# Attention rows kept turned into the MLP: the sums' reciprocals applied by a product, the mean taken out of the weights

## The chip, the cores and the metric

The kernel runs on one core of a Trainium2 chip. It has five engines with a queue each: PE (TensorE, matrix products; PEld is its weight load), DVE (VectorE), ACT (ScalarE), POOL (GpSimd) and SP (SyncE, which here only issues transfers). The metric is the device time of one execution in microseconds. The kernel before took 1570.1 us (median of 3 runs, 1569.33 to 1570.96).

## The reference

Attention over 8 batches and 8 heads of 576 rows and 64 columns, in which each row keeps its 32 largest scores, then a channel MLP with a residual on the 4608 rows of 512 columns that the heads give side by side.

```python
scores = scale * np.matmul(q, k.transpose(0, 1, 3, 2))
kth = np.partition(scores, -top_k, axis=-1)[..., -top_k:-top_k + 1]
scores = np.where(scores >= kth, scores, -1000000000.0)
scores = scores - np.max(scores, axis=-1, keepdims=True)
attn = np.exp(scores)
attn = attn / (np.sum(attn, axis=-1, keepdims=True) + 1e-09)
x = np.matmul(attn, v)                        # heads side by side: (8, 576, 512)
...
mu = np.mean(x, axis=-1, keepdims=True)
var = np.mean((x - mu) ** 2, axis=-1, keepdims=True)
xn = (x - mu) / np.sqrt(var + 1e-06) * g_ln
ch = np.maximum(xn @ w_ch1, 0.0) @ w_ch2      # 512 -> 2048 -> 512
return x + ch
```

q, k, v and g_ln are float32; the two weights come as float64 and are turned into float32 on the chip.

## The kernel before

**Units, groups, jobs.** A unit is 128 rows of scores for a pair of heads (or the last 64 rows of both heads, a *rest*). A job is one batch and one pair of heads with the row tiles worked on together; its units are its group. There are 160 units in 80 groups, in a written order: the first jobs have two whole units, in between stand jobs of a single rest, later ones have two whole units and a rest. Four jobs (the four pairs of heads) give the 512 columns of the same rows.

**A step.** A loop over steps n writes out each engine's instructions by hand, nothing is reordered later, and each queue runs in that order. In step n PE makes the scores of unit n+2 (`scores`, L438), ACT copies them out of PSUM (L419), DVE picks the 32 largest of unit n in four rounds (`select`, L483, L469, L475), with `halve` (L461, L462) ahead of the next unit. For unit n-1 ACT and POOL make the mask (`mask`, L532 on ACT, L535 on POOL) and ACT the exponential with its row sum (`weigh`, L543), which lands in the group's tile `den`; L555 adds the small constant. The weights are then turned: by PE and copies (`turn`, L606), or for "moved" units by a DVE transpose of 32x32 blocks (L577), a write to HBM (L594) and four reads back into `pt` (`bring`, L587). Some steps after its last unit, `lag`, a group meets the values: `values` (L669, L677) gives `av`, rows on the columns, head dimensions on the partitions.

**From values to the MLP.** `take_values` (L687) copies `av` to `oT`. `place` turns each 128 rows back on PE (L714) and ACT scales both heads' halves by the reciprocals in `den` (`put`, L691; the reciprocal is L1350 on DVE) into the tile `x`, rows on the partitions. Rests are gathered over two batches first (L705 on POOL), their sums moved by two small transfers (`keep_den`, L659), and are turned by `place_rest` (L721). When the four pairs are there, two tiles make a `Block` of 256 rows. `stats` (L742, L743) takes mean and variance on DVE, and POOL subtracts the mean from x (L748, L751; for the first block DVE does, L745). `turn_x` turns the centred rows again on PE (L778, copied by L781) into `xT`. Then come the hidden products (L819, ACT's relu L842) and the projection: plain for the first two blocks (L858), afterwards by the scheme of seven products in place of eight (`seven`, L979) with sums on POOL (L909 to L915, L959, L963). `finish` scales by the inverse deviation (L797), adds x (L790, POOL) and stores (L793).

**The planner.** PE's products of the blocks stand in a list `todo` of turns, hidden and projection products, with a cost each. Eight times in a step `fill` takes as many as the step's share allows (`slot`: the shares are evened out up to the next block, by costs per step, not by time). `give` puts a new block into the list: its turns ahead of the last ten projection products of the block before, its hidden products behind them. Turns wait until their rows are centred. Sums, ends, stores and transfers are put off by a number of fills (`Later`).

**Weights.** The 32 pieces of 128x512 are fetched and converted in steps -1 to 21 beside the attention: ACT (L164, L166, L169), POOL (L165, and for the first matrix L171, which multiplies the sign by the gain g), DVE (`shift`, L177), POOL (`join`, L183, L185). After that POOL makes the seven-product forms of the second matrix.

Of the kernel before, what the change touches and what calls it, by code (L numbers as in the profile page):

```python
# [21 lines left out]
J = 4  # L22
# [7 lines left out]
def compute(  # L30
# [52 lines left out]
    xtpool = pool("xt", 1)  # L83
# [26 lines left out]
    hi_homes = [const([P, 2, HALF + (1 if doubt is None else 2) * LOWS], f"hi{i}") for i in range(2)]  # L110
    ident = const([P, P], "ident")
    make_identity(nc, ident[:])
    columns = const([P, J + NC], "columns")
    half, gcol = columns[:, 0:J], columns[:, J : J + NC]
    nc.gpsimd.memset(half[:], -0.5)
    w1 = const([P, NC, DFF], "w1")
# [6 lines left out]
    class Piece:  # L123
# [22 lines left out]
        def fetch(self):  # L146
            self.raw = xpool.tile([P, DM, 2], U32, tag="x", name="raw")
            nc.sync.dma_start(self.raw[:].rearrange("p n w -> p (n w)"), self.src)

        def split(self):  # L150
            i = self.i
            high = self.raw[:, :, 1].bitcast(FP32)
            if i < 3 * NC:
                self.size = hpool.tile([P, DM], U32, tag="h", name="size")[:]
                self.low = wt_rows[:, i % 8]
                homes = ((opool, "o"), (opool, "o"), (rpool, "r"), (rpool, "r"), (xtpool, "xT"))
            else:
                self.size = wt_rows[:, 2 * i % 8].bitcast(U32)
                self.low = wt_rows[:, (2 * i + 1) % 8]
                homes = ((opool, "o"), (opool, "o"), (rpool, "r"))  # L160
# [9 lines left out]
            if self.i < NF:  # L170
                nc.gpsimd.tensor_scalar(  # L171
                    self.sign[:], self.sign[:], gcol[:, self.c : self.c + 1], 1.0,
                    ALU.mult, ALU.mult,
                )
# [6 lines left out]
        def join(self):  # L181
# [4 lines left out]
            ready[self.i] = now[0]  # L186
# [3 lines left out]
    ready = [None] * (2 * NF)  # L190
    pieces = [Piece(i) for i in range(2 * NF)]
# [3 lines left out]
    def load_gain():  # L195
        ps = turned()
        nc.tensor.transpose(ps[:, 0:NC], grow[:], ident[0:NC, 0:NC])
        nc.scalar.copy(gcol[:], ps[:, 0:NC])

# [337 lines left out]
    def weigh(u, t):  # L537
        g = u.group
        if g.den is None:
            g.den = denpool.tile([P, 2 * J + 1], FP32, tag="den", name="den")  # L540
        col = 2 * u.qt + t
# [5 lines left out]
        if u.rest:  # L547
            den = g.den[:, 2 * J : 2 * J + 1]
        elif u.weighed == 2 and u is [x for x in g.units if not x.rest][-1]:
            whole = [qt for qt in g.qts if qt < J]  # L550
            den = g.den[:, 2 * whole[0] : 2 * whole[-1] + 2]
            g.sums = den
        else:
            return
        nc.scalar.activation(den, den, AF.Copy, bias=DEN_EPS)  # L555
# [94 lines left out]
    xs, xps, rs, oTr, dr = {}, {}, {}, {}, {}  # L650
# [612 lines left out]
    for n in range(END):  # L1263
# [24 lines left out]
        if g and not quick:  # L1288
            values(g)
# [187 lines left out]
```

## Time and profile before

| | |
|---|---|
| runs | 1570.1 us (median of 3), 1569.33 to 1570.96 |
| profiled execution | 1571.11 us, its span 1569.2 us |
| granted clock of PE, mean over the span | 0.975 |
| PE, PEld busy | 1469.0 us (94%), 1108.0 us (71%) |
| DVE busy | 1363.4 us (87%) |
| ACT busy | 1083.8 us (69%) |
| POOL busy | 981.2 us (63%) |
| transfers | 374774 packets, 245.60 MB |

Busy times are shares of the whole span; the kernel has stages with different limits, so the prediction reads them by stretches. In a line of groups stand the source line, the engine, the operation, out<-in, the shapes and the count, then the busy time, the mean of one in ns, and the idle time of the engine just before with what ended it. In a timeline line stand start and length, the engine, line and tiles, and how many like it follow. PE's ends are modelled, and a product in float32 has two records.

### The profile page before, as it was taken

The page shows a single profiled execution, that of the slowest core. Times are in us where ns is not written, and L with a number is a line of the kernel's source. Part 1 is how long each engine was busy: PE and PEld are TensorE (multiplying, and loading weights), DVE is VectorE, ACT ScalarE, POOL GpSimd, SP SyncE. Part 2 cuts the span into 40 slices and gives each one's busy share as a digit, 9 for nine tenths or more (in the row PEclk, how much of TensorE's full clock was granted, in tenths as well). Part 3 has the DMA queues.
Part 4 walks back from the last instruction along what each step waited for, and adds up shares of the span by engine and source line. Part 5 has one row for each costly group of instructions (what it writes and reads, how often), then busy time and mean ns, then how long its engine had stood idle before and what let it go on. Part 6 is the DMA issues. An engine that isn't in the chain of part 4 may idle for free. (4 is left out here: it accounts for less than half of the span.)

```text
span 1569.2 us, 27215 instructions
## 1 busy us (share of the span) xinstructions
PE 1469.0 (94%) x8046; PEld 1108.0 (71%) x8046; DVE 1363.4 (87%) x3873; ACT 1083.8 (69%) x3081; POOL 981.2 (63%) x1318
## 2 busy tenths in 40 slices
PE   4568889999999999999999999999999998999997
PEld 3346446566787677778777777777777776788886
DVE  7997999899979998999988999999999999768000
ACT  6978887786777767767768676768676776555421
POOL 6968995747465565756566647474746475737524
PEclk9779989999999999999999999999999999999999
DMA  6623551466728865577754687657677557454511
GB/s 170 167 85 97 137 139 53 124 178 181 226 83 194 202 208 153 168 199 153 216 148 134 174 200 197 173 150 191 175 201 206 162 164 208 121 166 125 150 35 50
DMA packets 374774, 245.60 MB, mean 157 GB/s; under 512 B 255956, under 2 KB 343512, under 8 KB 374616
## 3 DMA queue, kind: packets, MB, share of 16 engines
q1 hardware_dynamic: 371048, 243.17, 57.6%
q8 instruction: 67, 1.10, 0.3%
q10 hardware_dynamic: 3568, 0.59, 0.3%
q14 instruction: 91, 0.75, 0.2%
HBM read 166.14 MB, written 77.53 MB: 155 GB/s over the span
## 5 line engine op out<-in xcount | busy, mean ns | idle before, releaser
L535 POOL TENSOR_TENSOR e<-e,sc 128x576 f32<-128x576 f32 x288 | 416.0, 1462 | 453.8 <-ACT e L532 392.9
L819 PE MATMUL hps<-xT,w 128*128 128x256 f32 x2304 | 542.2, 384 | 2.4 <-ACT xT L781 2.4
L819 PEld LDWEIGHTS hps<-xT,w 128*128 128x128 f32 x2304 | 423.0, 191 | 82.2 <-issue 27.2
L483 DVE MAX8 m<-hi 128x8 f32<-128x296 f32 (+1 forms) x1152 | 471.3, 444 | 1.2
L469 DVE MATCH_REPLACE8 hi<-m,hi 128x288 f32<-128x288 f32 (+1 forms) x864 | 377.0, 441 | 0.0
L979 PE MATMUL ops<-w,h 128*128 128x256 f32 x1280 | 304.8, 383 | 1.4 <-ACT o L944 1.4
L979 PEld LDWEIGHTS ops<-w,h 128*128 128x128 f32 x1280 | 233.6, 190 | 44.3 <-issue 13.5
L419 ACT COPY sc<-scps 128x288 f32<-128x288 f32 x576 | 188.5, 402 | 78.5 <-POOL e L535 56.2
L543 ACT ACTIVATE e<-e,m 128x576 f32<-128x576 f32 x288 | 225.1, 784 | 14.6 <-POOL e L535 12.5
L532 ACT ACTIVATE e<-sc,m 128x576 f32<-128x576 f32 x288 | 209.4, 769 | 0.0
L842 ACT ACTIVATE h<-hps 128x512 f32<-128x512 f32 x144 | 86.7, 602 | 114.1 <-PE hps L819 113.5
L577 DVE STREAM_TRANSPOSE sc<-e 128x1152 f32<-128x1152 f32 x87 | 118.8, 1366 | 52.5 <-ACT e L543 46.3
L669 PE MATMUL av<-pt,vb 128*64 128x256 f32 (+2 forms) x1280 | 148.8, 376 | 9.5 <-DMA pt<-turned 7.7
L462 DVE TENSOR_TENSOR lo<-sc 128x576 f32<-128x576 f32 (+1 forms) x160 | 136.1, 850 | 0.0
L461 DVE TENSOR_TENSOR hi<-sc 128x576 f32<-128x576 f32 (+1 forms) x160 | 130.0, 812 | 3.0 <-ACT sc L419 3.0
L669 PEld LDWEIGHTS av<-pt,vb 128*64 128x64 f32 x1280 | 81.6, 140 | 66.4 <-issue 17.1
L438 PE MATMUL scps<-kT,late_qT 64*128 64x288 f32 (+3 forms) x832 | 121.7, 410 | 0.2 <-ACT pt L618 0.2
L979 PE MATMUL ops<-wt,s 128*128 128x256 f32 x512 | 119.4, 383 | 0.0
L475 DVE MAX8 hi<-lo 128x8 f32<-128x288 f32 x288 | 117.5, 443 | 0.0
L438 PE MATMUL scps<-kT,qT 64*128 64x288 f32 x512 | 92.6, 460 | 23.5 <-DVE qT L366 8.0
L606 PE MATMUL tp<-ident,e 128*128 128x128 f32 x456 | 74.2, 290 | 39.9 <-ACT e L543 28.9
L979 PEld LDWEIGHTS ops<-wt,s 128*128 128x128 f32 x512 | 94.7, 190 | 17.3 <-issue 4.4
(111 smaller groups left out, 1793.5 us busy)
## 6 DMA issues: line engine op xcount, KB each, us to landing
turned<-sc SPq DMA_DIRECT2D x87, 576.0 KB, 4.2
pt<-turned SPq DMA_DIRECT2D x348, 144.0 KB, 3.2
w<-forms SPq DMA_DIRECT2D x128, 256.0 KB, 4.7
vb<-in_v_dram SPq DMA_DIRECT2D x80, 288.0 KB, 4.2
raw<-in_moe_w_ch_dram SPq DMA_DIRECT2D x32, 512.0 KB, 4.5
kT<-kept SPq DMA_DIRECT2D x48, 288.0 KB, 3.7
kept<-kT SPq DMA_DIRECT2D x32, 288.0 KB, 3.6
kqin<-in_k_dram SPq DMA_DIRECT2D x116, 72.0 KB, 2.6
```

The lines of the kernel that those rows point to most:

```text
L419: nc.scalar.copy(u.sc[:, t, s * HALF : (s + 1) * HALF], u.made[s][t][:, 0:HALF])
L438: nc.tensor.matmul(ps[i * R : i * R + ql, o : o + width], qT[r, q0 : q0 + ql], kT[r, k0 : k0 + width], start=True, stop=True,)
L461: nc.vector.tensor_tensor(hi, a, b, ALU.max)
L462: nc.vector.tensor_tensor(lo, a, b, ALU.min)
L469: nc.vector.match_replace(x, m[:, t, :], x, LOWEST)
L483: nc.vector.max(m[:, t, :], u.hi[:, t, r0 : r0 + width])
L532: nc.scalar.activation(u.e[:, t], u.sc[:, t], AF.Relu, bias=u.edge[:, t : t + 1], scale=-STEEP)
L535: nc.gpsimd.tensor_tensor(u.e[:, t], u.e[:, t], u.sc[:, t], ALU.subtract)
L543: nc.scalar.activation(u.e[:, t], u.e[:, t], AF.Exp, bias=u.bias[:, t : t + 1], scale=-scale, accum_out=g.den[:, col : col + 1],)
L669: nc.tensor.matmul(av[h * D : (h + 1) * D, 0 : g.nq], vb[:, h * (J + 1) + c, :], heads_of(g, h, 0, g.nq // 32)[:, :, c], start=(c == 0), s ...
L819: nc.tensor.matmul(ps[0][:, side * N : (side + 1) * N], w1[:, c, f * P : (f + 1) * P], self.xT[:, c, 0:N], start=(c == 0), stop=(c == NC - 1),
L979: nc.tensor.matmul(bank[name][:, 0:Q], a(j), rhs, start=first and j == 0, stop=(j == G - 1), skip_group_check=not first,)
```

## The change

The rows are no longer turned back ahead of the MLP.

- `keep_shares` takes the reciprocal of a group's sums, turns the 128x32 tile that holds them in 32x32 blocks on DVE, and SP sends each unit's row of 128 reciprocals to HBM (one transfer per tile of rows, 4, 5 or 1 per group). `fetch_shares` reads them back a step later, each row repeated over the 64 partitions of its head, into `shares`.
- `take_values` copies `av` straight to the place in `xT` (or, for rests, in `rest_xT`), and `place` multiplies it there by `shares` on POOL. So `xT` holds the unscaled-by-deviation, uncentred rows already turned, and the hidden products can read it. The two turns, the scalings on ACT, `place_rest`, `keep_den` and the centring on POOL go.
- The mean leaves the rows: every column of the first matrix (with g) gets its mean over the 512 inputs taken off. `load_gain` makes a tile `gmean` of -g/512; `means` multiplies four finished pieces by it on PE, and `centre`, a step later, forms g times piece plus that product on DVE in one pass per piece. POOL's product of sign and gain (L171) goes. A piece is ready when it is centred.
- `turn_x` turns `xT` to rows for the residual and the statistics, behind the first 24 hidden products of the block; `stats` follows a step later, `inverse` a step after that. The second turn of a block first writes out what is still put off of the block before.
- `give` appends to the list; buffers are shared out anew (three x tiles of 512 columns, three `xT`, two `rest_xT`; raw pieces and forms use the latter two kinds).

```diff
@@ pools
-    otpool = pool("ot", 1)
-    restpool = pool("ot_rest", 1)
+    sharepool = pool("shares", 1)
-    denpool = pool("den", 4)
-    xpool = pool("x", 4)
-    rpool = pool("r", 2)
+    denpool = pool("den", 1)
+    xpool = pool("x", 3)
-    xtpool = pool("xt", 1)
+    xtpool = pool("xt", 3)
+    restpool = pool("rest_xt", 2)
@@ Piece.split, load_gain
-            if self.i < NF:
-                nc.gpsimd.tensor_scalar(
-                    self.sign[:], self.sign[:], gcol[:, self.c : self.c + 1], 1.0,
-                    ALU.mult, ALU.mult,
-                )
...
+        for c in range(NC):
+            nc.scalar.mul(
+                gmean[:, c * P : (c + 1) * P], part[:].to_broadcast([P, P]), gcol[:, c : c + 1]
+            )
+    def means(n):
...
+        ps = product("mean")
+        for c in range(NC):
+            nc.tensor.matmul(
+                ps[:], gmean[:, c * P : (c + 1) * P], pieces[nb * NC + c].dst,
+                start=(c == 0), stop=(c == NC - 1),
+            )
+        return nb, ps
+    def centre(made, cs):
+        nb, ps = made
+        for c in cs:
+            x = pieces[nb * NC + c]
+            nc.vector.scalar_tensor_tensor(
+                x.dst, x.dst, gcol[:, c : c + 1], ps[:], ALU.mult, ALU.add
+            )
+            ready[x.i] = now[0]
@@ sums, values, place
+    def keep_shares(g):
+        nc.vector.reciprocal(g.sums, g.sums)
+        turned_den = denpool.tile([P, 32], FP32, tag="den", name="turned_den")
+        nc.vector.transpose(turned_den[:], g.den)
+        kept = g.kept = hbmpool.tile([2 * J + 1, P], FP32, tag="shares", name="shares")
+        n = g.sums.shape[1]
+        def send():
+            for c in range(n):
+                nc.sync.dma_start(
+                    kept[c : c + 1].rearrange("a (b q) -> (a b) q", q=32), turned_den[c : P : 32]
+                )
+        sends.add(send)
+    def fetch_shares(g):
+        t = g.shares = sharepool.tile([P, GQ], FP32, tag="shares", name="shares")
+        n = sum(qt < J for qt in g.qts)
+        for h in range(2):
+            rows = slice(h * D, (h + 1) * D)
+            if n:
+                nc.sync.dma_start(
+                    t[rows, 0 : n * P].rearrange("d (j p) -> d j p", p=P),
+                    g.kept[h : 2 * n : 2].unsqueeze(0).to_broadcast([D, n, P]),
+                )
...
     def take_values(g):
-        g.oT = otpool.tile([P, GQ], FP32, tag="oT", name="oT")
-        nc.scalar.copy(g.oT[:, 0 : g.nq], g.av[:, 0 : g.nq])
+        for to, cols in home_of(g):
+            nc.scalar.copy(to, g.av[:, cols])
     def place(g):
...
-            ps = brief("xo")
-            nc.tensor.transpose(ps[:, 0:P], g.oT[:, i * P : (i + 1) * P], ident[:])
-            put(xs[b, qt], ps, hp * P, g.den, 2 * qt)
+        for to, cols in home_of(g):
+            nc.gpsimd.tensor_tensor(to, to, g.shares[:, cols], ALU.mult)
@@ Block
-            nc.vector.bn_stats(out=st[:], in_=x)
+            nc.vector.bn_stats(out=st[:], in_=x[:])
             nc.vector.bn_aggr(out=self.mv[:, i, :], in_=st[:])
-                nc.gpsimd.tensor_scalar(x, x, 1.0, less[:], ALU.mult, ALU.add)
...
         def turn_x(self, i):
+            number = blocks.index(self)
+            if number and i == 1:
+                close(blocks[number - 1])
             tp = turned()
             for c in range(NC):
                 nc.tensor.transpose(
-                    tp[:, c * P : (c + 1) * P], self.x[i][:, c * P : (c + 1) * P], ident[:]
+                    tp[:, c * P : (c + 1) * P], self.xT[:, c, i * P : (i + 1) * P], ident[:]
                 )
+            x = self.x[i] = xpool.tile([P, DM], FP32, tag="x", name="x")
+            nc.scalar.copy(x[:], tp[:])
+            rows_of.setdefault(now[0] + 1, []).append((self, i))
@@ give and the step
-            todo[:] = kept + rows + last + hidden + project
+            todo.extend(hidden[:ROWS_AT] + rows + hidden[ROWS_AT:] + project)
...
+        averaged, fresh_means = fresh_means, means(n)
...
         if g and not quick:
+            fetch_shares(g)
             take_values(g)
...
+        settle_rows(n)
+        for x in recips.pop(n, []):
+            keep_shares(x)
+        settle_inverses(n)
```

More of the change, by code (lines that the diff above doesn't have):

```diff
@@ L546, in weigh @@
         )
[L547 to L555, printed above, removed]
+        if u is g.units[-1] and u.weighed == len(u.tiles):
+            n = 2 * len(g.qts) - u.rest
+            g.sums = g.den[:, 0:n]
+            nc.scalar.activation(g.sums, g.sums, AF.Copy, bias=DEN_EPS)
     def heads_of(g, h, i0, i1):
@@ L806, in rows @@
             return [
[L807 to L808 removed]
+                ("turn", 0.44, lambda i=i: self.turn_x(i), None) for i in range(self.n)
             ]
@@ L1329, in compute @@
         weights(n, 0)
+        weighed = ex if early else at(n - 2) if n - 2 >= EARLY else None
+        if weighed and weighed is weighed.group.units[-1]:
+            recips.setdefault(n, []).append(weighed.group)
         if early:
```

198 lines of the change are left out of this document (79 added, 119 removed).

## The prediction

> **What bounds the kernel now.** I read the busy time by stretches first, then one group's worth of work on the vector engine (DVE), then the groups by shape, the waits, and the transfers. The columns of the first view are the stretch, its length, and the busy time (and count) of PE, PEld, DVE, ACT and POOL, then the granted clock, the DMA share and GB/s.
>
> ```profile
> 20.00:100.00 80.00, 46.41 (x235) 32.20 (x237) 76.41 (x209) 69.98 (x191) 76.08 (x67) 0.76 0.49 137
> 100.00:240.00 140.00, 117.62 (x529) 71.85 (x526) 127.85 (x340) 116.61 (x297) 114.84 (x107) 0.91 0.44 115
> 240.00:840.00 600.00, 588.33 (x3479) 444.62 (x3478) 565.51 (x1637) 440.57 (x1300) 361.72 (x492) 0.99 0.62 165
> 840.00:1340.00 500.00, 490.46 (x2672) 372.33 (x2671) 497.46 (x1432) 356.92 (x1040) 304.07 (x447) 1.00 0.67 180
> 1340.00:1460.00 120.00, 120.00 (x627) 97.67 (x627) 80.99 (x218) 63.45 (x174) 71.82 (x105) 1.00 0.52 150
> 1460.00:1560.00 100.00, 99.17 (x487) 84.75 (x485) 5.00 (x14) 24.31 (x58) 43.64 (x84) 1.00 0.24 64
> ```
>
> There are four regimes. Up to 240 us weights are converted beside attention: DVE and POOL are both about 95% busy to 100 us and 91% and 82% after it, PE is not. From 240 to 1340 us DVE is at 96.6% of the time (1063.0 of 1100) and PE at 98% (1078.8), but PE's ends are modelled, so I ask which of the two never waits. From 840 on DVE is idle for 2.5 us in 500. From 1340 PE alone is full, and after 1460 DVE has nothing left.
>
> ```profile
> 1144.05 0.44 DVE L461 TENSOR_TENSOR hi<-sc 128x288 f32<-128x288 f32 x1
> 1167.66 0.44 DVE L461 TENSOR_TENSOR hi<-sc 128x288 f32<-128x288 f32 x1
> 280.00:300.00 20.00, 20.00 (x95) 11.55 (x94) 15.51 (x49) 16.46 (x46) 15.64 (x14) 1.00 0.44 147
> 420.00:480.00 60.00, 60.00 (x391) 47.27 (x388) 50.48 (x151) 44.18 (x137) 37.49 (x59) 1.00 0.48 137
> 580.00:640.00 60.00, 60.00 (x389) 47.27 (x388) 53.96 (x156) 46.01 (x144) 36.31 (x52) 1.00 0.55 154
> 700.00:720.00 20.00, 19.68 (x139) 15.22 (x140) 17.13 (x45) 13.49 (x44) 10.14 (x19) 1.00 0.67 149
> 800.00:840.00 40.00, 39.27 (x269) 31.45 (x268) 30.33 (x84) 28.73 (x94) 23.51 (x37) 1.00 0.36 104
> ```
>
> One group of three units takes DVE 23.61 us, from one such row to the other; over the 500 us around it DVE is 99.5% busy, so there each group lasts as long as its DVE work. The five stretches below them, 200 us, are those before 840 in which DVE waits (32.6 us) while PE is full: the steps of the 64-row rests and those behind a new block. So a microsecond on DVE counts in most of 240 to 1340, one on PE in those 200 us and from 1340 on.
>
> **The change part by part.** Prices first. The row of 1340 to 1560 is that of L714 alone (PE and PEld), the row of 240 to 1340 that of DVE's reciprocal L1350 alone; the L177 row gives the shortest, median and longest of its kind.
>
> ```profile
> 706.81 0.36 PEld L714 LDWEIGHTS xo<-ident,oT 128*128 128x128 f32 x2
> 707.13 0.73 PEld L819 LDWEIGHTS hps<-xT,w 128*128 128x128 f32 x4
> L714 PE MATMUL xo<-ident,oT 128*128 128x128 f32 x128 | 25.4, 279 | 5.0 <-ACT oT L687 3.9 <-ACT sc L419 1.0
> L721 PE MATMUL xo<-ident,oTr 128*128 128x128 f32 x16 | 4.4, 273 | 0.0
> 1340.00:1560.00 220.00, 2.67 (x14) 1.97 (x14) 1.00 0.40 111
> L858 PE MATMUL ops<-w,h 128*128 128x512 f32 x128 | 65.4, 641 | 0.3 <-POOL w L185 0.3
> 240.00:1340.00 1100.00, 8.65 (x65) 1.00 0.64 172
> L691 ACT ACTIVATE x<-xo,den 128x64 f32<-128x64 f32 x256 | 58.6, 311 | 17.2 <-DVE den L1350 9.5 <-PE xo L714 7.5
> 1148.32 0.74 DVE L366 STREAM_TRANSPOSE kT<-kqin 128x576 f32<-128x576 f32 x1
> 1148.99 0.40 DVE L366 STREAM_TRANSPOSE qT<-kqin 128x256 f32<-128x256 f32 x1
> L742 DVE BATCH_NORM_STATS2 st<-x 128x6 f32<-128x512 f32 x32 | 21.5, 673 | 38.2 <-ACT x L691 38.2
> L745 DVE TENSOR_SCALAR x<-x,mv 128x512 f32<-128x512 f32 x2 | 1.0, 487 | 0.1
> L177 DVE TENSOR_SCALAR wt<-wt x20: 408/822/1630, 114.3 to 232.1; 128x512 uint32<-128x512 uint32 x20
> L171 POOL TENSOR_SCALAR sign<-sign,columns 128x512 f32<-128x512 f32 x16 | 17.0, 1065 | 3.4 <-ACT sign L169 1.6 <-ACT m L495 0.8
> L751 POOL TENSOR_SCALAR x<-x,less 128x512 f32<-128x512 f32 x30 | 24.8, 826 | 3.1
> L963 POOL TENSOR_TENSOR o<-o,t 128x256 f32<-128x256 f32 x32 | 25.3, 792 | 14.0 <-ACT t L953 14.0
> L790 POOL TENSOR_TENSOR o<-o,x 128x512 f32<-128x512 f32 x32 | 41.4, 1304 | 21.2 <-ACT o L797 21.2
> ```
>
> *PE.* The 144 turns of the attention rows (L714, L721) go; the turns of x stay, with their operands swapped. Two such turns take the array from 706.81 to the next load at 707.13, 0.16 us each, 23 us in all. 14 lie behind 1340, where PE sets the end: 2.2 us. The 200 us of full PE hold few, since the groups of rests have one turn for two groups: some 20, an estimate, 3.2 us. The others lie beside a full DVE and give nothing. PE: -5, with bounds of 0 and -23. The 16 mean products of 512 columns are added before 240 us; L858's 128 records are 64 products, and two records of 641 ns overlap, so 4 products are at most 5.1 us in a step where PE has a third of its time free. I cost them at nothing; if that cover is gone they cost up to 20.
>
> The Trainium skill's Trace Analysis page, under Identifying the Most-Contended Engine, says to judge TensorE by its weight-load busy share and not by matmul busy, and to work on the engine of the highest occupancy; that is DVE here (PEld 372 of 500 us, DVE 497), and by it the whole PE term is 0, the third rival below. The trace agrees with it from 840 to 1340 and not behind 1340, where DVE is idle.
>
> *DVE, each group.* The reciprocals stay one per group (80 for 80). A 128x32 transpose of the sums is added, 80 times. From 0.40 us at 256 columns and 0.74 at 576 a line gives 0.16 at 32; as it reads what the reciprocal has just written, I take 0.2 (bounds 0, where it falls in a wait, and 0.40). 65 reciprocals run between 240 and 1340 us; less the 16 groups of rests alone, 49 count: +9.8 (0 to 26).
>
> *The early stage.* POOL loses 16 products of the sign and the gain (-17.0 us) and gains a product per group for nine groups (9 x 0.79 = +7.1): -10. DVE gains 16 passes over a 512-column weight piece with a PSUM operand, of which no row exists; nearest are 0.487 and 0.673, and the contended 0.822. I take 0.67: +10.7 (0.487 to 1.63 each: 8 to 26). It loses two subtractions (-1.0) and the wait before its first statistics, and gains nine transposes (+1.8). As POOL and DVE are both near full here, and ACT with them (70 of 80), POOL's 10 us come out only as far as DVE lets them: I take +4, with bounds of -10 and +17. W1 pieces are usable two steps later; block 0's later products wait for W2 pieces to step 20 in any case, so that costs nothing.
>
> The Trainium skill's SBUF page, under Who interferes with whom, says that only the second port pair of DVE is shared with GpSimd, exclusively; a pass with one PSUM operand would then not be held up as L177 is in its slow cases. By it the passes would be the 10.7 taken and not the 13.2 of the contended median. No run here shows such a pass.
>
> *ACT* loses 256 scalings (58.6 us) and 32 of the rests and keeps its copies; it is 71% busy in 840 to 1340 and bounds nothing there. *Rows turned back later.* The hidden products no longer wait for statistics, centring and a turn of x; but the ten products kept over from the block before cover that chain now, so it gives nothing. The second turn of a block first closes the block before it, and ACT's copy may then wait for a residual on POOL (1.3 us); 24 hidden products stand ahead, so I cost it at nothing, and at 18 x 1.3 = 23 us without that cover. The mean's removal from x takes 30 POOL passes of 826 ns away and brings 64 of about 792 ns for the shares: no change of weight, but of place.
>
> *The shares' way.* That place is the open part.
>
> ```profile
> 1154.19 1.78 SPq L587 DMA_DIRECT2D pt<-turned  x4
> 1156.49 0.43 SPq L380 DMA_DIRECT2D kept<-late_qT  x1
> 1155.92 0.43 ACT L687 COPY oT<-av 128x320 f32<-128x320 f32 x1
> 1156.41 0.24 POOL L705 COPY oTr<-oT 128x64 f32<-128x64 f32 x1 [2.46 <-ACT oT L687]
> 1161.32 1.48 POOL L535 TENSOR_TENSOR e<-e,sc 128x576 f32<-128x576 f32 x1 [4.68 <-ACT e L532]
> 1153.84 0.70 ACT L419 COPY sc<-scps 128x288 f32<-128x288 f32 x2 [1.59 <-POOL e L535]
> pt<-turned SPq DMA_DIRECT2D x348, 144.0 KB, 3.2
> dr<-den SPq DMA_DIRECT2D x64, 0.2 KB, 2.8
> SPq L587 <- DMA turned<-sc: 198.2, 61, 6.8
> POOL e L535 <- ACT e L532: 392.9, 111, 10.2
> ```
>
> SP gets 416 more issues (288 sends, 192 fetches, less 64) at about 0.45 us: 187 us spread over a queue that mostly waits (198 us behind one kind alone). The fetch stands behind the bring (L587) and the kept heads. In this group it would be issued from 1156.9, four of them to 1158.7, and land 3.2 us later at 1161.9; the products (0.79 and some 0.5) end at 1163.2, and the mask that starts at 1161.32 starts 1.9 us later. Behind the mask are ACT's copies of scores and its exponential, and then DVE, but a step ahead of need. Bounds: 0, and 65 x 1.9 = 124 if every one reached DVE. POOL has 393 us of waiting for ACT at that very row, so I stay near the low end: +3. A fetch also waits on SP for its own sends (2.8 us), issued half a step before; behind it on SP are the load of values and the next turned block, which have a step to spare.
>
> *At the end* PE's last products, two evacuations and the residual sums are as before. **Sum:** -5 +9.8 +4 +3 = +11.8 on the profiled execution's own 1571.1 us, 1582.9; that execution is 1.0 above the median of 1570.1, so I predict **1582**.
>
> **The rivals.** *PE is the bound all along, and it gets faster.* For it: PE shows 490 of 500 us. Then the 126 turns from 240 us on are worth 20.2 us and DVE's additions fall into waits: 1570.1 - 20 = 1550. It decides once over 17 of those 20 us reach the end. Against it: 2.5 us of DVE idle time in 500. *The shares hold POOL.* If a quarter of the 124 us reaches DVE, 31 stand for 3: 1610. For it: ACT already waits 1.59 us for a mask at 1153.84. *The turns give nothing:* where PE waits for nothing it may be paced by the planner's shares, which the change leaves; then the 5 us fall out: 1587. For it: PEld is at 372 of 500 us. *It cancels out:* the transpose lies in waits that the late statistics leave (38.2 us of DVE waiting for x rows): 1570.
>
> **How the numbers follow.** Forecast 0.32, the turns giving nothing 0.14, the shares 0.17, PE the bound 0.24, cancelling 0.13. About 3.1 us (0.2%) is what a measurement tells apart. Faster takes 0.24 and a little of the forecast's low end (0.25), within 0.2% 0.13, slower 0.62. The forecast's own range, with the third rival, is 1574 to 1592; with half of the fast case and two thirds of the held one the range is 1556 to 1606.
>
> **What would show it.** The group of three units lasting 23.8 us, not 23.6, with DVE still over 99% busy from 840 to 1340, shows the DVE term; PE no shorter there shows the turns hidden. New waits of POOL for the shares' landing, and longer ACT waits for masks, would show the third. Passes over weights longer than 0.8 us, or the 240 us mark moved by more than 10 us, would upset the early term. DVE idle by more than 5% in 840 to 1340 would make the whole reading wrong.

## The result and the profile after

The changed kernel takes 1586.22 us (median of 4 runs, 1584.9 to 1587.67); the kernel before took 1570.53 us beside it. The ratio is 1.010, with a 95% interval of 1.0083 to 1.0118: slower by 15.7 us. I had forecast 1582, within 1556 to 1606. The sign and the size came out. Of the terms behind them, the early stage had the wrong reasons, and the way of the shares and the rows turned back later were too small; they partly cancelled, which was luck.

The stretches of the changed kernel, in the columns of the prediction's first view (length; PE, PEld, DVE, ACT, POOL busy; clock, DMA share, GB/s):

```profile
20.00:100.00 80.00, 47.06 (x229) 31.30 (x229) 72.31 (x191) 62.87 (x166) 58.72 (x56) 0.76 0.43 121
100.00:240.00 140.00, 119.95 (x548) 73.32 (x547) 139.55 (x368) 116.48 (x285) 120.93 (x110) 0.93 0.45 127
240.00:840.00 600.00, 577.11 (x3318) 432.41 (x3317) 568.26 (x1673) 407.46 (x1144) 362.40 (x481) 0.97 0.60 169
840.00:1340.00 500.00, 489.70 (x2629) 371.76 (x2629) 488.86 (x1401) 336.23 (x944) 305.85 (x436) 0.99 0.64 182
1340.00:1460.00 120.00, 120.00 (x625) 97.59 (x622) 101.08 (x268) 62.97 (x164) 81.08 (x113) 1.00 0.55 166
```

PE shows 577 us in 240 to 840 where it had 588: it waits more often. DVE is full from 100 to 240 us now (139.6 us of 140, where it had 127.9). Its idle time from 840 to 1340 is 11.1 us, and it was 2.5; but the same work comes later now, and a wait of 5.5 us at 849.74 falls into this stretch; the kernel before has its like (4.6 us at 833.70) just ahead of it. So I also took both kernels between the same two pieces of work, from the halving of the 93rd unit to that of the 149th, first before and then after:

```profile
847.24:1303.63 456.39, 450.78 (x2450) 340.38 (x2449) 454.02 (x1310) 330.34 (x968) 281.74 (x419) 1.00 0.68 181
862.88:1329.46 466.58, 456.28 (x2422) 344.63 (x2422) 461.30 (x1328) 312.39 (x878) 289.97 (x417) 0.99 0.65 183
```

This part is 10.2 us longer; 7.3 of them are more DVE work, 2.9 are DVE waits. DVE's work also reaches past 1340: 101.1 us are left for 1340 to 1460, where 81.0 were. ACT is less busy than before nearly everywhere, POOL only up to 100 us. So behind 240 us no engine has become a new bound: DVE has more work, and more waits.

The waits, who waited for whom (total us, times, longest), of DVE, POOL and ACT in the changed kernel:

```profile
DVE turned_den L675 <- DMA shares<-turned_den: 21.6, 7, 6.1
DVE dens L673 <- ACT dens L577: 11.5, 6, 5.2
POOL e L562 <- ACT e L559: 230.7, 92, 7.1
POOL xT L749 <- DMA shares<-shares: 166.5, 36, 9.7
ACT sc L446 <- POOL e L562: 64.2, 26, 6.2
ACT x L793 <- POOL o L800: 24.0, 16, 5.6
```

Four of these are new. DVE's transposition of the sums (L675) waits until the sends of the group before have read its one buffer. All seven of these waits lie between 435 and 817 us. The reciprocal (L673) waits for ACT's sums. POOL's product by the shares (L749) waits for their fetch, and what it waits there comes out of the 392.9 us that POOL waited for ACT before. ACT's copy of the rows turned back (L793) waits for a residual sum (L800), because the turn closes the block before.

The first of the new waits as it looks in the trace, SP's issues and then DVE's instructions (start, length, form, and in brackets the idle time before it):

```profile
428.29 1.31 SPq L693 DMA_DIRECT2D shares<-shares  x2
429.70 0.53 SPq L365 DMA_DIRECT2D vb<-in_v_dram  x1
430.27 1.62 SPq L1058 DMA_DIRECT2D w<-forms  x3
432.00 2.14 SPq L681 DMA_DIRECT2D shares<-turned_den  x4
...
429.60 0.15 DVE L673 RECIPROCAL dens<-dens 128x1 f32<-128x1 f32 x1
435.80 0.21 DVE L675 STREAM_TRANSPOSE turned_den<-dens 128x32 f32<-128x32 f32 x1 [6.05 <-DMA shares<-turned_den]
```

The sends stand on SP behind a fetch, values and three weight forms; they go out at 432.0, the last at about 434.1, and DVE, which had its reciprocal done at 429.75, goes on at 435.8. This is a stretch of 64-row rests: the group that waits is one short unit (its sums are 128x1), and its sums come before the four rows of the group before it have left.

### The profile page after: what moved, and what is told of

The parts are those of the page before. It is cut to its first block, busy times and chain, and to the rows that moved or that the text cites. A ratio compares the mean times of both kernels' runs of the same rounds, so it can differ in the third digit from the quotient of the medians.

```text
span 1585.1 us, 27404 instructions
## 1 busy us (share of the span) xinstructions
PE 1475.0 (93%) x7934; PEld 1108.6 (70%) x7934; DVE 1394.2 (88%) x3967; ACT 1029.1 (65%) x2797; POOL 985.3 (62%) x1300
## 3 DMA queue, kind: packets, MB, share of 16 engines
q1 hardware_dynamic: 391784, 252.75, 56.2%
## 4 chain that ended last, share of the span: by engine, by line
PE 45%; DVE 34%; DMA 6%; POOL 5%; ACT 4%; SPq 2%; issue 2%; DVEq 0%; ACTq 0%; POOLq 0%
PE hps L825 17%; PE ops L986 15%; DVE m L510 10%; DVE hi L496 9%; PE av L710 4%; PE scps L465 4%; DVE sc L599 3%; DVE lo L489 3%; DVE hi L488 3%; DVE hi L502 3%; POOL e L562 2%; PE tp L628 1%; DMA pt<-turned 1%; DMA turned<-sc 1%; PE av L718 1%
## 5 line engine op out<-in xcount | busy, mean ns | idle before, releaser
L825 PE MATMUL hps<-xT,w 128*128 128x256 f32 x2048 | 486.6, 388 | 1.2 <-DVE w L222 1.2
L825 PEld LDWEIGHTS hps<-xT,w 128*128 128x128 f32 x2048 | 383.1, 193 | 77.4 <-issue 25.0
L986 PE MATMUL ops<-w,h 128*128 128x256 f32 x1280 | 299.7, 383 | 1.9 <-ACT o L951 1.9
L446 ACT COPY sc<-scps 128x288 f32<-128x288 f32 x576 | 189.4, 403 | 89.4 <-POOL e L562 64.2
L570 ACT ACTIVATE e<-e,m 128x576 f32<-128x576 f32 x288 | 224.2, 781 | 18.4 <-POOL e L562 15.9
L749 POOL TENSOR_TENSOR xT<-xT,shares 128x256 f32<-128x256 f32 x64 | 51.9, 811 | 245.5 <-DMA shares<-shares 166.5
L489 DVE TENSOR_TENSOR lo<-sc 128x576 f32<-128x576 f32 (+1 forms) x160 | 141.9, 887 | 0.0
L710 PEld LDWEIGHTS av<-pt,vb 128*64 128x64 f32 x1280 | 81.8, 141 | 68.2 <-issue 20.4
L465 PE MATMUL scps<-kT,qT 64*128 64x288 f32 x512 | 95.9, 466 | 29.4 <-ACT qT L380 8.1
```

What stands on the lines that cost most here:

```text
L446: nc.scalar.copy(u.sc[:, t, s * HALF : (s + 1) * HALF], u.made[s][t][:, 0:HALF])
L465: nc.tensor.matmul(ps[i * R : i * R + ql, o : o + width], qT[r, q0 : q0 + ql], kT[r, k0 : k0 + width], start=True, stop=True,)
L489: nc.vector.tensor_tensor(lo, a, b, ALU.min)
L570: nc.scalar.activation(u.e[:, t], u.e[:, t], AF.Exp, bias=u.bias[:, t : t + 1], scale=-scale, accum_out=g.den[:, col : col + 1],)
L710: nc.tensor.matmul(av[h * D : (h + 1) * D, 0 : g.nq], vb[:, h * (J + 1) + c, :], heads_of(g, h, 0, g.nq // 32)[:, :, c], start=(c == 0), s ...
L825: nc.tensor.matmul(ps[0][:, side * N : (side + 1) * N], w1[:, c, f * P : (f + 1) * P], self.xT[:, c, 0:N], start=(c == 0), stop=(c == NC - 1),
```

## The experiments

All times below are medians; the kernel before took 1570.1 to 1571.2 us beside each of them, so they can be set against one another within a microsecond. Theory: DVE's work per group and the rests of the shares' way cost, as the prediction's sum has it. Rivals: PE sets the pace all along, the shares hold POOL, the turns give nothing, the new work falls into waits.

**One buffer or two for the turned sums.**

```diff
-    denpool = pool("den", 1)
+    denpool = pool("den", 2)
...
+                both = small.tile([P, 3, 2], FP32, tag="mv", name="mv")
+                self.mv, self.rstd = both[:, 0:2], both[:, 2]
```

The two small tiles of the statistics become one in the same edit.

> The tile of turned sums gets a second buffer (nothing is left out). Before it the changed kernel takes 1586.2 us, and DVE waits 21.6 us in it for a group's sends to release that one buffer. If DVE sets the pace up to 1340 us, that wait goes and the time falls by 5 to 15 us, since about half of what such a wait costs is given back a few steps later: 1571 to 1581. If PE sets the pace, or if the price is the transposition itself and not the wait for its buffer: 1584 to 1587.

1581.12 us, 5.1 less than the changed kernel (ratio to the kernel before 1.0073, 1.0055 to 1.0091). The intervals of the two overlap a little, but five of the six runs lie below the lowest of the changed kernel. The wait is gone from the list; a part of it comes back as longer waits for the sums themselves, which were 11.5 us:

```profile
DVE dens L673 <- ACT dens L577: 19.6, 7, 5.8
```

A quarter of the 21.6 us reached the end. A wait of DVE does cost here, so DVE counts, and most of it is given back.

**Without the transposition.**

```diff
+    ones = const([P, 32], "ones")
+    nc.gpsimd.memset(ones[:], 1.0)
...
-        turned_den = denpool.tile([P, 32], FP32, tag="den", name="turned_den")
-        nc.vector.transpose(turned_den[:], g.den)
+        turned_den = ones
```

> DVE's transposition of the sums is left out: the sends read a tile of ones that is written once, so the shares of the output are wrong. Reciprocals, sends, fetches and products stay. DVE theory: 65 groups from 240 to 1340 us at 0.30 us each, and the 21.6 us of waits for its buffer, are on the path; 10 to 25 us less than the changed kernel, 1561 to 1576. Theory that PE sets the pace, or that the shares' landing holds POOL and through it DVE: 0 to 3 us less, 1583 to 1586.

1574.91 us, 11.3 less (ratio 1.0026, 1.0014 to 1.0039). If 5.1 of this is the buffer's wait, 6.2 are the work's; that is an estimate, since SP's sends, which wait 116.5 us for the transposition in the changed kernel, no longer wait for DVE either. In place of that wait DVE waits longer for ACT's sums (11.5 us in the changed kernel):

```profile
DVE dens L675 <- ACT dens L579: 20.4, 8, 6.0
```

The group of three units of the prediction, from one row of its kind to the other, in the changed kernel:

```profile
1164.97 0.44 DVE L488 TENSOR_TENSOR hi<-sc 128x288 f32<-128x288 f32 x1
1187.99 0.21 DVE L675 STREAM_TRANSPOSE turned_den<-dens 128x32 f32<-128x32 f32 x1
1188.84 0.44 DVE L488 TENSOR_TENSOR hi<-sc 128x288 f32<-128x288 f32 x1
```

It lasts 23.87 us with the transposition, 23.61 without the change. With the transposition left out it is back at 23.63. So the price is 0.25 us per group where DVE never waits: 0.21 us for the instruction and the rest behind the reciprocal.

**Without the fetches.**

```diff
+    sames = const([P, GQ], "sames")
+    nc.gpsimd.memset(sames[:], 1.0)
...
-        t = g.shares = sharepool.tile([P, GQ], FP32, tag="shares", name="shares")
+        g.shares = sames
+        return
```

> The fetches of the shares from HBM are left out: the products on POOL multiply by a tile of ones that is written once, so the output lacks the division. Reciprocals, transpositions and sends stay. POOL's 166.5 us of waiting for shares to land go. Theory that the shares hold POOL: 10 to 31 us less, 1555 to 1576. DVE theory: the masks start earlier but are needed a step later; 0 to 4 us less (my term was 3), 1582 to 1586.

1574.15 us, 12.1 less (ratio 1.0021, 1.001 to 1.0031). The DVE theory had 0 to 4. The fetches cost four times my term, and the rival that the shares hold POOL has the right size, at its low end. POOL's wait for the landing is replaced by its old one, and DVE's wait for its buffer shrinks by 8.9 us; SP has 192 issues less to make ahead of the sends:

```profile
DVE turned_den L676 <- DMA shares<-turned_den: 12.7, 5, 3.8
...
POOL e L563 <- ACT e L560: 423.1, 132, 8.5
```

**The turns given back to PE.**

```diff
             nc.gpsimd.tensor_tensor(to, to, g.shares[:, cols], ALU.mult)
+        for i, qt in enumerate(g.qts):
+            if qt < J or g.job.b % 2:
+                ps = brief("xo")
+                nc.tensor.transpose(ps[:, 0:P], ident[:], ident[:])
```

> PE gets the 144 turns of 128x128 back that the change took away, at the place where the products by shares are issued; they turn the identity matrix and nobody reads them (nothing of the result is left out). Forecast's term: 5 us more, 1591. Turns hidden wherever the planner paces PE: 0 to 1 us more, 1587. PE the bound all along: 20 us more, 1606. The comparison of the two traces behind 1303 us, where the changed kernel wins 10 us back, speaks for 7 to 10 us more, 1594 to 1596.

1589.2 us, 3.0 more (ratio 1.0114, 1.0096 to 1.0133). 20 us are excluded: PE is not the bound all along. Between my 5 and the 0 of a hidden PE the run does not decide sharply, as the intervals of this kernel and of the changed one overlap. PE's granted clock differs as well: 0.972 to 0.977 in these runs, 0.963 to 0.970 in the changed kernel's. Over the 60 runs of the kernel before beside these experiments, 0.01 of clock goes with 2.7 us in the mean, so by this estimate some 2 us of the turns' price may be hidden, not 17. And these turns read nothing that is late, so they bring back PE's work and not its old waits. The expectation's last line, 7 to 10 us, is wrong: what the changed kernel wins at its end is not the turns (see below).

**Neither transposition nor fetch.** Both edits together.

> Transposition and fetches are both left out: sends read a tile of ones, the products on POOL multiply by ones; reciprocals stay. Alone these two brought 11.3 and 12.1 us. If they are separate costs (DVE's work in every group; landings and SP's queue ahead of POOL's products), the two add up: 20 to 24 us less than the changed kernel, 1562 to 1566, faster than the kernel before. If both only remove the same wait of the transposition for its buffer: 12 to 15 us less, 1571 to 1574.

1558.42 us, 27.8 less than the changed kernel and 12 less than the kernel before (ratio 0.9928, 0.9912 to 0.9945). The two costs are separate and a little more than additive (23.4): with the fetches out, the transposition costs 15.7 us and not 11.3. Alone, each leaves DVE waits that the other causes: 20.4 us for the sums with the transposition out, 12.7 us for the buffer with the fetches out. With both out 10.3 us are left (the first line), and between the 93rd and the 149th unit DVE is idle for 2.5 us, as it was before the change (the second):

```profile
DVE dens L676 <- ACT dens L580: 10.3, 5, 4.9
```

```profile
839.65:1298.70 459.05, 451.91 (x2419) 340.95 (x2419) 456.60 (x1307) 310.97 (x878) 287.89 (x419) 0.99 0.64 180
```

So the transposition and the fetches of the shares cost 27.8 us, and everything else in the change, the sends and POOL's products among it, gains 12.

**The rows turned back behind more products.**

```diff
-    SEND_AGE, PLACE_AGE, ROWS_AT = 1, 1, 24
+    SEND_AGE, PLACE_AGE, ROWS_AT = 1, 1, 40
```

> The turns of x back into rows stand behind 40 of a block's 64 hidden products and no longer behind 24 (nothing is left out). In the changed kernel ACT waits 24.0 us, 16 times, at the copy of the turned rows for POOL's residual sum of the block before, and DVE is idle behind it at 1118 us. If closing the block before at the turn costs time on the path: ACT's wait goes and 3 to 8 us are won, 1578 to 1583. As forecast, closing at the turn costs nothing: 1585 to 1587.

1578.97 us, 7.3 less (ratio 1.0059, 1.0045 to 1.0074). I had costed closing the block at the turn at nothing, because 24 products stand ahead; they do not cover it everywhere. ACT's wait for the residual falls from 24.0 to this:

```profile
ACT x L793 <- POOL o L800: 11.0, 8, 3.0
```

How such a wait travels can be followed at 1104 to 1118 us of the changed kernel, POOL first, then ACT, then DVE:

```profile
1108.00 0.73 POOL L749 TENSOR_TENSOR xT<-xT,shares 128x256 f32<-128x256 f32 x1 [7.11 <-ACT sc L446]
1108.97 2.78 POOL L562 TENSOR_TENSOR e<-e,sc 128x576 f32<-128x576 f32 x2
1113.53 2.70 POOL L800 TENSOR_TENSOR o<-o,x 128x512 f32<-128x512 f32 x2
...
1108.29 0.61 ACT L793 COPY x<-tp 128x512 f32<-128x512 f32 x1
1115.04 0.59 ACT L793 COPY x<-tp 128x512 f32<-128x512 f32 x1 [5.59 <-POOL o L800]
1116.03 0.78 ACT L570 ACTIVATE e<-e,m 128x576 f32<-128x576 f32 x1
1117.24 0.78 ACT L570 ACTIVATE e<-e,m 128x576 f32<-128x576 f32 x1
...
1118.21 1.38 DVE L599 STREAM_TRANSPOSE sc<-e 128x1152 f32<-128x1152 f32 x1 [2.12 <-ACT e L570]
```

POOL is idle for 7.1 us at the product by the shares. The view names ACT's copy as the last releaser, but the last fetch of the shares was issued only at 1105.26, 2.7 us ahead of the product; that its landing ends the wait is inferred. The masks and the residual sums follow late. ACT's second copy waits 5.6 us for the residual, the exponentials stand behind that copy, and DVE's transposition of e waits 2.1 us for them. Three things stand in this chain: a late fetch, a product ahead of the masks, and a copy that waits ahead of the exponentials. The wait of 2.1 us is gone without the fetches, and it is gone with 40 products. Yet it is the only wait of this kind that DVE shows between the 93rd and the 149th unit, and most of what 40 products win lies elsewhere: 12.4 us between the 41st and the 93rd unit (435.3 us against 447.7), among the rests, where DVE's waits for its one buffer fell from 21.6 to 14.9 us. How far those hang on the closing was not separated.

**The products by the shares at the end of the step.**

```diff
-        if g and not quick:
-            place(g)
         fill()
...
+        if g and not quick:
+            place(g)
         if g and not quick and g.job.hp == NHP - 1:
```

> The products by the shares are issued at the end of their step, some half a step later (4 us) on POOL's queue (nothing is left out). If the shares' landing costs by holding POOL in front of the masks: most of POOL's 166.5 us of waiting goes, and of the 12.1 us that leaving the fetches out brought 5 to 10 come back, 1576 to 1581. If the fetches cost by their places on SP's queue (late sends, late loads): 0 to 2 us, 1584 to 1587.

1577.94 us, 8.3 less (ratio 1.0052, 1.0038 to 1.0066). Moving POOL's instruction alone, with every transfer where it was, brings two thirds of what leaving the fetches out brought. That does not show that two thirds of the fetches' price are the wait at POOL, because the two gains lie at different places of the profiled executions. By the 21st unit this kernel is 4.1 us ahead of the changed one, and the one without fetches is 0.4 behind it. From the 41st to the 93rd unit, with the rests, this one wins 4.8 and that one 8.2; from the 93rd to the 149th this one loses 2.1 and that one wins 4.8. At the place followed above, the product still stands ahead of the next masks, and DVE's wait of 2.1 us is still there (at 1112.20). How the fetches' price divides between POOL's wait and the places on SP's queue stays open. Half of POOL's wait is left:

```profile
POOL xT L749 <- DMA shares<-shares: 86.3, 22, 7.2
```

**The weights' part alone**, in the kernel before.

```diff
-            if self.i < NF:
-                nc.gpsimd.tensor_scalar(
-                    self.sign[:], self.sign[:], gcol[:, self.c : self.c + 1], 1.0,
-                    ALU.mult, ALU.mult,
-                )
...
-                nc.gpsimd.tensor_scalar(x, x, 1.0, less[:], ALU.mult, ALU.add)
...
+        averaged, fresh_means = fresh_means, means(n)
...
+            centre(averaged, (0, 1))
...
+            centre(averaged, (2, 3))
```

> The kernel before with the mean's removal in the weights alone: 16 products of the sign and the gain go, 16 mean products on PE and 16 passes on DVE come, the rows of x are no longer centred; shares, xo turns and the order of work stay as they were (nothing is left out). My early term is +4 against the kernel before; the centring of x that goes (30 POOL passes) was costed at nothing: 1572 to 1576. The rival: POOL freed of 10 us early and of the passes over x later, and the products no longer waiting for the centring: 3 to 10 us less, 1560 to 1567.

1565.14 us, 5.6 less than the kernel before beside it (ratio 0.9967, 0.9954 to 0.998). This is the rival's value. In the stretch to 100 us, this kernel beside the kernel before (76.41 us of DVE, 76.08 of POOL, clock 0.76):

```profile
20.00:100.00 80.00, 52.55 (x253) 35.14 (x255) 79.32 (x214) 71.08 (x193) 63.39 (x57) 0.84 0.49 143
```

POOL is 13 us less busy, DVE does 79.3 us of work in 80, and PE gets 6 us more done, but the attention is not ahead yet: the halving of the 9th unit starts 2.2 us later than before. The gain comes behind it, and that of the 17th unit starts 3.5 us earlier. DVE's waits for POOL's weight pieces, 8.9 us of them from 122 to 142 us in the kernel before, suggest why. The first line is of the kernel before, the second of this one:

```profile
DVE wt L177 <- POOL wt L165: 9.3, 6, 3.4
```

```profile
DVE wt L173 <- POOL wt L166: 0.5, 3, 0.2
```

POOL had been late for DVE there, so its relief came out although DVE was nearly full: the passes took the place of waits. The halving of the 21st unit, one piece of work in all kernels, starts at 229.88 us before, 227.04 here, 232.49 in the changed kernel and 227.82 in the one with neither transposition nor fetch. The weights' part gains 2.8 us early; that the changed kernel is 2.6 us late there is the doing of transposition and fetches together (with one of them left out it is still 2.4 or 3.0 us late). At the 149th unit 1.2 us of the gain are left (1302.46 against 1303.63), and the rest is won behind it, where PE had some 4 us of waits before and has under 1 here. What took these waits away was not tried by itself.

**The sums taken off DVE altogether** (two kernels). The second leaves the products and the turns of x where the change put them; the first adds the two moves above.

```diff
-        nc.vector.reciprocal(g.sums, g.sums)
-        turned_den = denpool.tile([P, 32], FP32, tag="den", name="turned_den")
-        nc.vector.transpose(turned_den[:], g.den)
+        nc.gpsimd.tensor_tensor(g.sums, g.sums, half_less[:, 0 : g.sums.shape[1]], ALU.pow)
...
-                nc.sync.dma_start(
-                    kept[c : c + 1].rearrange("a (b q) -> (a b) q", q=32), turned_den[c : P : 32]
-                )
+                nc.sync.dma_start(kept[c : c + 1].rearrange("a b -> b a"), sums[:, c : c + 1])
```

> The changed kernel with the shares' way off DVE (nothing is left out): the reciprocals are a power of -1 on POOL, each column of sums is sent as it lies (128 pieces of 4 bytes) and not turned, the products by the shares stand at the end of their step, and x is turned back behind 40 hidden products. If DVE's pace and POOL's waits are what the shares cost: 11 us for the transposition, 7 and 8 us for the two moves, and some 10 us for the reciprocals (65 of 164 ns between 240 and 1340 us), overlapping in part: 1550 to 1562, faster than the kernel before. If the small pieces land late and hold POOL in place of the fetches, or the power on POOL holds the masks: 1566 to 1578.

> Only the reciprocals on POOL and the columns sent unturned (nothing is left out); the products and the turns of x stay where the change put them. DVE's pace: 11 us for the transposition and its buffer and 5 to 10 us for the reciprocals, 1565 to 1571. If the power on POOL or the small pieces hold POOL: 1574 to 1584.

1937.64 and 2077.54 us (ratios 1.2328 and 1.325): both rivals of the expectations were too mild by hundreds of microseconds. In the second kernel, the power on POOL as a group (count, busy us, mean ns, idle before), and then what SP and POOL waited for:

```profile
L674 POOL TENSOR_TENSOR dens<-dens 128x4 f32<-128x4 f32 (+2 forms) x80 | 79.3, 991 | 1.7 <-ACT dens L578 1.7
```

```profile
SPq L680 <- POOL dens L674: 269.5, 63, 26.4
SPq L610 <- DMA turned<-sc: 221.2, 46, 11.9
SPq L690 <- DMA shares<-dens: 105.6, 20, 9.3
POOL xT L746 <- DMA shares<-shares: 536.2, 51, 16.7
```

The power takes 0.99 us in the mean, mostly for four columns, where DVE's reciprocal takes 0.16. It stands in POOL's queue behind products that wait for shares. The sends on SP wait for the power, and all other transfers stand behind the sends: 269.5 us, up to 26.4 at a time. That closes a ring: POOL waits for fetches, the fetches for sends, the sends for POOL. The sends also read the tile of sums itself now, and ACT's exponentials, which write their sums into it, wait 78.3 us for them. How much of the loss is the ring and how much the landing of 128 pieces of 4 bytes was not separated.

**The power on POOL without shares.** The kernel with the weights' part alone, its reciprocals as a power.

```diff
-            nc.vector.reciprocal(den, den)
+            nc.gpsimd.tensor_tensor(den, den, less_one[:, 0 : den.shape[1]], ALU.pow)
```

> The kernel before with the mean out of the weights (1565.1 us) and its reciprocals as a power of -1 on POOL (nothing is left out). If DVE sets the pace: 79 reciprocals of 134 and 119 ns and what stands between them, 5 to 10 us less: 1555 to 1560. If POOL's place in its queue counts more, since the power waits for ACT's sums ahead of the masks: 1563 to 1568.

1594.54 us, 29.4 more than without it (ratio to the kernel before 1.0154, 1.0141 to 1.0167). Both values expected were too low. What the power adds to POOL's queue costs more than DVE's 80 short reciprocals, early above all: the halving of the 21st unit starts 19.6 us later. ACT's scalings wait for the power, and DVE waits again for POOL's weight pieces, 23.2 us where it was 0.5:

```profile
ACT x L718 <- POOL den L1368: 37.6, 7, 7.5
DVE wt L175 <- POOL wt L168: 23.2, 13, 4.4
```

**Three mends of the change together.** Two buffers, 40 products, and the products by the shares later: at the end of the step for the last pair of heads, behind the next step's masks for the others.

```diff
-    denpool = pool("den", 1)
+    denpool = pool("den", 2)
...
-    SEND_AGE, PLACE_AGE, ROWS_AT = 1, 1, 24
+    SEND_AGE, PLACE_AGE, ROWS_AT = 1, 1, 40
...
+            if g.job.hp == NHP - 1:
+                place(g)
+            else:
+                to_place.append(g)
...
+        while to_place:
+            place(to_place.pop())
```

> The changed kernel with three mends (nothing is left out): two buffers for the turned sums, x turned back behind 40 hidden products, and the products by the shares issued later, at the end of their step for the last pair of heads of a batch element and behind the next step's masks for the other three. Alone the first brought 5.1 us, the second 7.2, the move to the end of the step 8.3. If they are separate costs: 1562 to 1567, faster than the kernel before. If they are the same waits seen three times: 1575 to 1580. DVE's 0.25 us per group for the transposition stays in either case.

1572.92 us, 13.3 less than the changed kernel (ratio to the kernel before 1.0012, 1.0001 to 1.0022). That lies between the two theories: alone the three brought 20.7, the third of them in a milder form, so at least a third would be the same time seen twice. POOL's wait for the landing is down from 166.5 to this:

```profile
POOL xT L749 <- DMA shares<-shares: 34.5, 12, 7.0
```

The 14.5 us that are left over the kernel with neither transposition nor fetch were not taken apart; the group of three units still lasts 23.87 us, so DVE's 0.25 us per group are among them. The best kernel of all that leave nothing out is the one with the weights' part alone, 1565.1 us.

## Why the prediction was right, and where it was not

*What bounds.* DVE as the pace holds where it never waits: taking 0.25 us per group off it shows in full in the group's length, and 144 turns more on PE cost 3.0 us of the 20 that the PE rival had. PE was no shorter from 840 to 1340 (489.7 us, 490.5 before), as I had said of hidden turns. My sign "DVE over 99% busy from 840 to 1340" failed at 97.8%, in good part because work and its waits come later and shift into the stretch: between the 93rd and the 149th unit DVE is 98.9% busy.

*It cancels out.* This rival had the new work fall into DVE's waits for rows of x. In part it did: four such waits between 436 and 808 us, 15.3 us, shrink to 1.1, and the waits for the one buffer, 21.6 us, stand in about the same places. The stretch of the rests, from the 41st to the 93rd unit, is 13.2 us longer even so.

*PE, -5.* 3.0 measured, not clearly apart from 0. The Trainium skill's Perfetto Trace Analysis page, under Identifying the Most-Contended Engine, would have it at 0; these runs do not rule that out.

At the end the changed kernel nevertheless wins time back. The same piece of work, the halving of the 149th unit, and the busy times from there to the end of the span, first before and then after:

```profile
1303.63 0.75 DVE L462 TENSOR_TENSOR lo<-sc 128x576 f32<-128x576 f32 x1
```

```profile
1303.60:1569.20 265.60, 251.65 (x1281) 208.51 (x1279) 122.22 (x332) 111.07 (x293) 138.52 (x216) 0.99 0.42 119
```

```profile
1329.46 0.75 DVE L489 TENSOR_TENSOR lo<-sc 128x576 f32<-128x576 f32 x1
```

```profile
1329.50:1585.10 255.60, 245.31 (x1245) 204.21 (x1243) 124.90 (x338) 101.71 (x254) 137.50 (x210) 0.99 0.43 128
```

It is 25.8 us late there and 15.9 at the end. PE has 36 products and turns less to do, 6.3 us busy, of which only 17 are turns of the attention rows; the others (products of scores and projections) it had done already, as DVE was late and PE was not. Before, PE also waited some 4 us in this stretch. So about ten microseconds of DVE's loss never reach the end, which my sum did not have.

*DVE, each group, +9.8.* 0.2 us taken, 0.25 measured in the group's length; times the 49 groups that is 12.3. Leaving the transposition out brought 11.3, of which 5.1 belong to the wait for its buffer, so by this estimate only about half of the work's price reached the end while the fetches were there (without them the same edit brought 15.7). The wait was not in my term, the part given back was not either; the bounds (0 to 26) held both.

*The early stage, +4.* The number came near by luck: at the 21st unit the changed kernel is 2.6 us late. The term put the weights and the shares of the first nine groups together, and taken apart they have opposite signs. The weights' part alone is 2.8 us early there and gains 5.6 in all; transposition and fetches cost 4.7 there (232.49 against 227.82). The failed step is that POOL's 10 us come out only as far as a full DVE lets them. DVE was waiting for POOL's pieces, and those waits went while its passes came. The price of the pass was right:

```profile
L222 DVE SCALAR_TENSOR_TENSOR w<-w,columns,mean 128x512 f32<-128x512 f32 x16 | 11.1, 731 | 0.0
L212 PE MATMUL mean<-w,gmean 128*128 128x512 f32 x32 | 14.8, 605 | 0.0
```

11.1 us against the 10.7 taken. All 16 lie between 702 and 735 ns, beside shifts that take from 408 to 1629 ns in the same stretch. That agrees with the Trainium skill's SBUF — State Buffer page, under Who interferes with whom: a DVE instruction with at most one SBUF input, outside the modes that use both port pairs, does not contend with GpSimd, and the second input of these passes lies in PSUM. The mean products, costed at nothing, stayed so as far as the early starts show.

*The shares' way, +3.* The failed size: the fetches cost 12.1 us alone. Of the prediction's step, "a step ahead of need" was not true everywhere: at 1104 to 1118 us the chain POOL, ACT, DVE had less than a step of slack, for 2.1 us of DVE. The larger part of the price came where I had not looked, having read one ordinary group: 8.2 us of it lie from the 41st to the 93rd unit, where the sends stand behind the fetches on SP and DVE waits for its buffer (21.6 us, 12.7 without fetches). The sign that I named for the rival, new waits of POOL for the landing, stands at 166.5 us, and ACT's waits for masks went from 56.2 to 64.2.

*Rows turned back later, 0.* Wrong by 7.3 us: the cover of 24 products that I named is not enough, and the bound of 23 was the right place to look. The path of most of these 7.3 us is open, as said above.

*The sum.* Measured: weights -5.6 (in the kernel before), transposition and fetches +27.8, all else -6.5 (what is left of +15.7 if the parts add up). Predicted: +4, then +9.8 and +3 for the shares, then -5. A gain of the weights that I took for a loss and some 15 us of the shares' waits that I took for 3 stand against each other; that the total came within 4.2 us is in good part luck.

*The clock.* PE was granted 0.963 to 0.970 in the changed kernel and 0.967 to 0.979 in the kernel before. By the 2.7 us per 0.01 above, that goes with some 2 of the 15.7 us, an estimate; it is not what made the difference.

## What to carry to other kernels

A product that waits for a transfer belongs behind everything on its queue that others wait for; moving one instruction of POOL to the end of its step was worth 8.3 us here, though not at the place that I had followed. A single buffer between an engine and sends on a busy queue makes the engine wait for that queue where groups are short, so look at the shortest groups and not at the ordinary one. When two engines are both nearly full, ask which of them the other's idle time waits for before deciding that relief of one is worth nothing.

## What the runs showed of the hardware

A power on POOL takes 991 ns in the mean for mostly four columns of 128 rows, six times DVE's reciprocal of the same sums (163 ns). A 128x32 transposition on DVE takes 212 ns, and 0.25 us of a group's time behind the reciprocal that it reads. I had not expected sends that wait for POOL to cost so much: with 80 small powers, 79 us of work, and 288 column sends behind them the kernel was 491 us slower than the changed one, and its mean granted clock 0.869 where it was 0.963.
